# A tile scheduler that models the port between VectorE and GpSimd, small products for two columns, an early table load, and four wide stages

## Chip, core and metric

The kernel runs on one core of a Trainium2 chip. The time is the device time of one execution in microseconds (us), the median over several executions. Lower is better.

## What is computed

An RWKV-style attention feeds a two-layer block with a leaky ReLU. Shapes: 4 batches, 8 heads, 768 steps, head width 48; 3072 tokens of width 384; hidden width 2048.

```python
# attention, for each step t, state starts at zero
cur   = einsum('bhd,bhe->bhde', u[None] * k_t, v_t)
y_t   = einsum('bhd,bhde->bhe', r_t, state + cur)
state = w[None, :, :, None] * state + einsum('bhd,bhe->bhde', k_t, v_t)
# x is y with the heads side by side: [3072, 384]
h = x @ w_in                    # 384 -> 2048
out = maximum(0.01 * h, h) @ w_out   # 2048 -> 384
```

## The kernel before

**Tiling.** The 24 stages (4 batches x 6 chunks of 128 steps) are numbered n = 0 to 23. Stage n is one attention chunk and yields 128 tokens. Inside a chunk the recurrence is written with powers of w: r and k are multiplied by tables (`tab`, L786), scores are taken on TensorE (`sc`, L898), masked on VectorE (`at`, L916), multiplied with v and with the carried state (`y`, L928 and L932), the bonus term with u is added (`ys`, L939), and the new state is formed (`kv` L951/L955, `s` L964). The result is turned to have features on partitions (`yt`, L976, evicted by `xt`, L982; from stage 10 on by a transposing DMA, L987).

**Two forms of a stage.** A plain stage loads r, k and v with 192-byte rows (L619), and multiplies 128x768 in one VectorE instruction (`kq`, L786); eight TensorE transposes (`tp`, L832) give `kt`. The first `NWIDE` = 5 stages are "wide": they are loaded in 1536-byte rows (L617), in an order in which eight consecutive steps of one head lie in one partition. Those need other tables (`tabw`, L582 and L586, made from `lnp`, L578, the logarithm of a narrow load of w, L538), a multiplication for r and one for k (`kw`, L743), a turn of r, k and v by 16 small products each (`turn`, L714), and back-transposes `bk` (L767) and `bv` (L807). In wide stages the bonus comes from a product with the columns `uw` (`pq` L857, `pb` L864, `b` L869/L870, `bv` L873), in plain ones from two GpSimd multiplications and a VectorE reduction (`pu` L880, `pr` L882, `b` L884, `bv` L886).

**Columns.** `wcol` and `uw` hold w and u along partitions. Two ScalarE-queue DMAs load w and u into `wu` (L654, L655) and two fp32 transposes turn them (L600, L601). The ScalarE table load (L1151) stands after those DMAs.

**The hidden block.** `moe_g1` (L1015) multiplies `xT` with `w_in` in blocks of one PSUM bank; `ga` (L1029) evicts a block to `gring`; for every 2 or 4 blocks `gs` makes 0.01*h (L1043 on VectorE, L1044 on ScalarE) and `gm` takes the maximum (L1050, VectorE). `moe_g2` (L1077) multiplies with `w_out` in four quarters per stage; `ob` (L1088, L1089) evicts, and a DMA writes the output (L1094). `GROUPS` says how many stages share one `g1`: single stages 0 to 3, then pairs, and single stages 22 and 23. The last stage's `g2` is cut in 3 column parts.

**What sets the order.** Nothing is written out by hand: `Plan.schedule` (L136) places all operations. Each has an engine or several to choose from (`alt`), a planned duration, dependencies, buffers, and a priority made of its due time and an offset by kind (`POFF`). At each step an engine takes the candidate that can begin first, ties by priority. The engines then run their lists in order, each waiting on semaphores (`sync`, L380). TensorE lists are filled with products of zeros (L1114) where the planner expects idle time before `WARM_UNTIL` = 20 us. `Plan.execute` (L260) replays the lists with a model of the DMA queues for the planned landing times. `DMA_SEQ` writes the order of the first loads: `st2@r0` issues the loads of stage 2 once r of stage 0 has landed; `wi0`, `wi1` are the two halves of w_in and `wo0` to `wo2` the parts of w_out, on GpSimd's queue.

Of the kernel before, what the change touches and what calls it, by code (L numbers as in the profile page):

```python
# [6 lines left out]
ALU = mybir.AluOpType  # L7
AF = mybir.ActivationFunctionType
AX = mybir.AxisListType
BF16 = mybir.dt.bfloat16  # L10
# [14 lines left out]
GROUPS = [1, 1, 1, 1, 2, 2, 2, 2, 2, 2, 2, 2, 2, 1, 1]  # L25
# [11 lines left out]
HEAD_SLACK = 0.1  # L37
HEAD = 14.0
POFF = {'pb': -6, 'tab': -6, 'b': 6, 'xt': -12, 'g1': 12, 'bv': 12, 'vw': -1.5, 'vb': -6, 's': -6, 'bdw': 6, 'kv': -12, 'vt': -1.5, 'sc': 1.5, 'af': -12, 'kt': -3, 'kq': 1.5, 'pu': -6, 'tp': -1.5, 'g2': -6, 'ys': -6, 'od': 12, 'at': 1.5, 'tv': 6, 'gs': 3, 'uw': -3, 'bk': 3, 'pr': -6, 'wc': 3, 'ln': -12, 'yt': -6, 'pq': -1.5, 'ob': -1.5}
# [6 lines left out]
WI = [8, 8]  # L46
WO = [4, 4, 8]
DMA_SEQ = 'st0 st1 st2@r0 u@k0 w@r0 st3@k0 wi0@v2 wi1@v3 wo0@u st4@v0 wo1@v0 wo2@r1'
WP_ON = "SP"
NWIDE = 5  # L50
V_WIDE = 5
BONUS_PE = 5
MASK_SPLIT = 0
KT_SPLIT = 2
KQ_SPLIT = 1
GS_POOL = 0
LAST_SPLIT = 3
GA_ALT = 8
# [4 lines left out]
class Op:  # L63

    def __init__(self, eng, took, fn, name, prio):
        self.alts = [(eng, took, fn)]
        self.eng, self.fn, self.name, self.prio = eng, fn, name, prio
        self.deps, self.behind, self.vals, self.new, self.users = set(), set(), [], [], []
        self.pk, self.sem, self.ndma = None, None, 1
        self.start = self.end = self.done = self.pos = self.semval = None  # L70
        self.left = 0
        self.mark = False
        self.snap, self.waits = {}, []
        self.count = 1
# [27 lines left out]
class Plan:  # L102
# [5 lines left out]
    def op(self, eng, took, fn, name, prio, reads=(), writes=(), after=(), pk=None, sem=None, ndma=1,  # L108
           behind=(), joins=(), alt=None):
# [4 lines left out]
        o.pk, o.sem, o.ndma = pk, sem, ndma  # L114
# [21 lines left out]
    def schedule(self, filler, filler_dep, filler_until):  # L136
# [40 lines left out]

        left = len(self.ops)
        while left:
            pick = None  # L180
            for e in ENGS:
                best = None
                for o, al in cand[e]:
# [14 lines left out]
                    if sl is None:  # L198
                        continue
                    key = (max(st, free[e] + (HEAD_SLACK if free[e] < HEAD else SLACK)), o.prio)  # L200
# [34 lines left out]
            free[e] = o.end  # L235
            if o.pk is not None:
                if o.name in self.landing:
                    o.done = o.end + self.landing[o.name] + (MARGIN if o.name[:2] in ("ld", "wi", "wo") else 0.0)
                else:
                    dma_free[0] = max(o.end + 1.0, dma_free[0]) + o.pk[0] * o.pk[1] / 16000.0  # L240
                    o.done = dma_free[0] + LAND
# [18 lines left out]
    def execute(self, order, case=(1.6, 1.0, 1.1, 2.4, 0.7, 1.0)):  # L260
# [7 lines left out]
        hold = {}  # L268
        now = 0.0
# [14 lines left out]
        def advance():  # L284
            moved = True
            while moved:
                moved = False
                for e, lst in order.items():
                    while nxt_i[e] < len(lst) and e not in hold:
# [23 lines left out]
                        else:  # L313
                            end[o] = st + took - min(HIDE[e], took / 2)
# [5 lines left out]
        def issue(o, e, fin):  # L320
# [3 lines left out]
            begin[o] = fin + (gap_w if e == "POOL" else gap_h if heavy else gap_l + (0.0 if any(x in end for x in dmaq[e][:1] if x is not o) else 0.5))  # L324
# [96 lines left out]
def bass_rwkv5_eagle__then__act_leaky_relu_kernel(  # L421
# [13 lines left out]
    def SB(name, shape, dt=BF16):  # L435
        return ctx.enter_context(nc.sbuf_tensor(name, shape, dt))
# [12 lines left out]
    lnw = SB("lnw", [128, H, D], FP32)  # L449
    lnp = SB("lnp", [128, D], FP32)  # L450
# [5 lines left out]
    wu = SB("wu", [HP, 2, 2, 64], FP32)  # L456
    id4 = SB("id4", [HP, HP], FP32)
# [47 lines left out]
    def build(landing):  # L505
# [17 lines left out]
        def pr_a(n, x=0.0):  # L523
            return (n - LEAD) * PERIOD + x

        f_ones, f_tri, f_idn, f_bd, f_zer, f_uw, f_bdw, f_wc, f_wc2, f_lnw, f_lnw2, f_u, f_wu, f_id4 = [
            fixed(x) for x in ("ones", "tri", "idn", "bd", "zer", "uw", "bdw", "wc", "wc2", "lnw", "lnw2", "u", "wu", "id4")]
# [6 lines left out]
        f_lnp, f_lnp2, f_row, f_rowf = [fixed(x) for x in ("lnp", "lnp2", "row", "rowf")]  # L534
        f_cj = [fixed(f"cj{x}") for x in range(2)]
        f_tabw = [[fixed(f"tabw{i}{x}") for x in range(2)] for i in range(2)]
        if NWIDE:
            o_wp = op(WP_ON, 0.7, lambda: [ENG[WP_ON].dma_start(lnp[:, :], dram(w, 0, [[0, 16], [D, H], [1, D]]))],  # L538
                      "wp", -201, writes=[f_lnp], pk=(128, 16.3), sem="wp")
        o_zer = op("DVE", 0.2, lambda: V.memset(zer[:, :], 0.0), "zer", -200, writes=[f_zer])  # L540
        op("DVE", 0.17, lambda: V.memset(ones[:, :], 1.0), "ones", -199, writes=[f_ones])
        op("DVE", 0.17, lambda: V.memset(wu[:, 0, :, :], 1.0), "wu0", -198, writes=[f_wu])
        op("DVE", 0.17, lambda: V.memset(wu[:, 1, :, :], 0.0), "wu1", -197, joins=[f_wu])
        op("DVE", 0.07, lambda: V.memset(id4[:, :], 1.0), "id40", -196, writes=[f_id4])
        for i, (base, mul) in enumerate([(-L, 1), (L - 1, -1), (0, 1), (-1, -1)]):
# [9 lines left out]
        op("POOL", 0.15, lambda: G.affine_select(id4[:, :], id4[:, :], pattern=[[1, HP]], compare_op=ALU.is_equal,  # L555
                                                 fill=0.0, base=0, channel_multiplier=-1),
           "id4", -193, writes=[f_id4])
# [6 lines left out]
        if NWIDE:  # L564
# [13 lines left out]
            op("ACT", 0.2, lambda: A.activation(lnp[:, :], lnp[:, :], AF.Ln), "lnp", -196, reads=[f_lnp], writes=[f_lnp2])  # L578
            for i in range(min(2, NWIDE)):
                for x in range(2):  # L580
                    def mtw(eng, i=i, x=x):
# [3 lines left out]
                       reads=[f_lnp2, f_cj[x]], writes=[f_tabw[i][x]], alt=("POOL", 1.1, (lambda mtw=mtw: mtw(G))) if i else None)  # L585
# [13 lines left out]
        def go_tuw():  # L599
            PE.transpose(puw.t[:, 0:HP], wu[:, 0, :, :].rearrange("p a d -> p (a d)"), id4[:, :])  # L600
            return PE.transpose(puw.t[:, HP:2 * HP], wu[:, 1, :, :].rearrange("p a d -> p (a d)"), id4[:, :])  # L601
# [3 lines left out]
        def load(n, prio, after=()):  # L605
# [3 lines left out]
            for xi, (nm, src) in enumerate((("r", r), ("k", k), ("v", v))):  # L609
                fv = fixed(f"{nm}{n}")  # L610

                wide = n < NWIDE and (xi < 2 or n < V_WIDE)
# [40 lines left out]
        def go_wu():  # L653
            return [A.dma_start(wu[:, 0, :, 0:D], dram(w, 0, [[2 * D, HP], [D, 2], [1, D]])),  # L654
                    A.dma_start(wu[:, 1, :, 0:D], dram(u, 0, [[2 * D, HP], [D, 2], [1, D]]))]  # L655
        op("ACT", 1.4, go_wu, "wu", -400, writes=[f_wu], pk=(60, 30), ndma=2, sem="wu")
# [39 lines left out]
        op("PE", 0.1, go_tuw, "tuw", -150, reads=[f_wu, f_id4], writes=[puw]).count = 2  # L696
# [11 lines left out]
        op("DVE", 0.56, lambda: mbdw(V), "bdw", -18, reads=[f_bd, f_wc2], writes=[f_bdw], alt=("POOL", 1.1, lambda: mbdw(G)))  # L708
# [16 lines left out]
        def attention(n):  # L725
# [11 lines left out]
            if n < NWIDE:  # L737
                kw_ = new("kw", n)
                for x in range(2):
                    kws = {"writes": [kw_]} if x == 0 else {"joins": [kw_]}  # L740

                    def mw(eng, x=x):
# [4 lines left out]
                            reads=[(f_r, f_k)[x], f_tabw[l][x]], alt=("POOL", 1.15, (lambda mw=mw: mw(G))) if n else None, **kws)  # L747
# [13 lines left out]
                bk = bank(f"a_bk{n}")  # L761

                def go_bk():
                    o = None
                    tv = bk.t[:, :].bitcast(BF16)
                    for i in range(HP):
                        o = PE.transpose(tv[:, 128 * i:128 * i + 128], kt.t[:, HP + i, :], idn[:, :])  # L767
                    return o
                q = op("PE", 0.22, go_bk, f"bk{n}", pr_a(n, 0.47), reads=[f_idn], writes=[bk], after=[ev])
                q.count = HP  # L770
                kt.readers.append(q)

                def cpb(e):
                    o_ap = kq.t[:, H:2 * H, :].rearrange("p h e -> p (h e)")
                    i_ap = bk.t[:, :].bitcast(BF16)[:, 0:512]
                    return V.tensor_copy(o_ap, i_ap) if e == "DVE" else A.activation(o_ap, i_ap, AF.Copy)
                op("DVE", 0.42, lambda: cpb("DVE"), f"kq{n}", pr_a(n, 0.48), reads=[bk] + f_pad, writes=[kq],
                   alt=("ACT", 0.6, lambda: cpb("ACT")))
            elif n < KQ_SPLIT:
                for x in range(2):  # L780
# [3 lines left out]
                           f"kq{n}_{x}", pr_a(n, 0.0), reads=[(f_r, f_k)[x], f_tab[l][x]] + f_pad, **kw))  # L784
            else:
                use(op("DVE", 1.2, lambda: V.tensor_tensor(kq.t[:, :, 0:D], vr.t[:, 0:2, :, :].rearrange("p a h d -> p (a h) d"),  # L786
                                                           tab[l][:, :, :, :].rearrange("p a h d -> p (a h) d"), ALU.mult),
                       f"kq{n}", pr_a(n, 0.0), reads=[f_r, f_k] + f_tab[l] + f_pad, writes=[kq]))
            vb = new("vb", n)
            if n < NWIDE and n < V_WIDE:  # L790
                vw, vt, tv_, bv_ = new("vw", n), new("vt", n), bank(f"a_tv{n}"), bank(f"a_bv{n}")
                def cw(e):
# [4 lines left out]
                       alt=[("DVE", 0.35, lambda: cw(V)), ("POOL", 0.7, lambda: cw(G))]))  # L797
# [56 lines left out]
            if n < max(BONUS_PE, NWIDE):  # L854
                pq, pb = new("pq", n), bank(f"a_pb{n}")
                def mpq(eng):
                    return eng.tensor_tensor(pq.t[:, :, :], kt.t[:, 0:HP, :], kt.t[:, HP:2 * HP, :], ALU.mult)  # L857
                op("DVE", 0.48, lambda: mpq(V), f"pq{n}", pr_a(n, 0.38), reads=[kt], writes=[pq],
                   alt=("POOL", 1.4, lambda: mpq(G)))
# [12 lines left out]
                def mbv(eng):  # L872
# [4 lines left out]
                   alt=("POOL", 1.1, lambda: mbv(G)))  # L877
            else:
                pu, pr, bb = new("pu", n), new("pr", n), new("b", n)
                use(op("POOL", 1.15, lambda: G.tensor_tensor(pu.t[:, :, :], vr.t[:, 1, :, :], ubc[:, :, :], ALU.mult),  # L880
                       f"pu{n}", pr_a(n, 0.2), reads=[f_k, f_u], writes=[pu]))
                use(op("POOL", 1.15, lambda: G.tensor_tensor(pr.t[:, :, :], pu.t[:, :, :], vr.t[:, 0, :, :], ALU.mult),  # L882
                       f"pr{n}", pr_a(n, 0.3), reads=[f_r, pu], writes=[pr]))
                op("DVE", 0.54, lambda: V.tensor_reduce(bb.t[:, :], pr.t[:, :, :], AX.X, ALU.add),  # L884
                   f"b{n}", pr_a(n, 0.8), reads=[pr], writes=[bb])
                op("POOL", 1.1, lambda: G.tensor_tensor(bv.t[:, :].rearrange("p (h d) -> p h d", d=D),  # L886
                                                        vb.t[:, :].rearrange("p (h d) -> p h d", d=D),
                                                        bb.t[:, :].unsqueeze(2).to_broadcast([128, H, D]), ALU.mult),
                   f"bv{n}", pr_a(n, 0.4), reads=[vb, bb], writes=[bv])
# [100 lines left out]
        def moe_g1(n0, T):  # L990
# [16 lines left out]
            for j in range(NFB // per):  # L1007
# [25 lines left out]
                if j % nu == nu - 1:  # L1033
# [12 lines left out]
                    def mx(j0=j0, j=j, hv=hv):  # L1046
# [4 lines left out]
                    op("DVE", 0.79 if nu == 4 else 0.46, (lambda sc=sc: sc("DVE")), f"gs_{n0}_{j}", pr + 0.07,  # L1051
                       after=parts[-nu:], writes=[hv],
                       alt=[("ACT", 1.92 if nu == 4 else 1.06, (lambda sc=sc: sc("ACT")))]
                       + ([("POOL", 2.6 if nu == 4 else 1.4, (lambda sc=sc: sc("POOL")))] if n0 < GS_POOL else []))
                    m = op("DVE", 1.38 if nu == 4 else 0.76, mx, f"gm_{n0}_{j}", pr + 0.08, reads=[hv], after=parts[-nu:])
# [163 lines left out]
```

## Time and profile before

| | |
|---|---|
| median of 5 runs | 182.13 us (181.94 to 182.59) |
| the profiled execution's own time | 182.85 us |
| span of that execution, first to last instruction | 181.1 us |
| mean granted TensorE clock | 0.981 |
| busy: TensorE, VectorE, ScalarE, GpSimd | 171.2, 154.7, 114.9, 82.5 us |
| first `g1` product (L1015) begins | 27.52 us |
| last TensorE product ends | 178.7 us |
| DMA moved | 28.07 MB, mean 155 GB/s |

The profile is of one execution. A line of the groups gives source line, engine, operation, output and input tiles, count, busy time and mean time of one. The timeline lists instructions by start and length; consecutive ones can overlap by their fill and drain, so distances between starts are what one costs its engine. "Idle before" names what ended a wait. Products of zeros count as TensorE busy time.

### The profile page before, as it was taken

How to read it: one execution, taken by the hardware profiler on the slowest of the kernel's cores; microseconds unless marked ns; L12 is line 12 of the kernel's file. 1: busy time of each engine (PE TensorE's matmuls, PEld its weight loads, DVE VectorE, ACT ScalarE, POOL GpSimd, SP SyncE). 2: the span in 40 equal slices, each digit the busy share in tenths (PEclk: the TensorE clock that was granted, in tenths of full speed). 3: DMA queues.
4: the chain of work that ended last, by engine and by line, in shares of the span. 5: the costliest groups of instructions: out<-in, count | busy, mean ns of one | idle time of the engine just before them, and what ended most of it. 6: DMA issues, size and time to landing. Idle time of an engine off the chain costs nothing.

```text
span 181.1 us, 4983 instructions
## 1 busy us (share of the span) xinstructions
PE 171.2 (95%) x2084; PEld 134.3 (74%) x2084; DVE 154.7 (85%) x225; ACT 114.9 (63%) x175; POOL 82.5 (46%) x88
## 2 busy tenths in 40 slices
PE   7388998999999999999999999999999999999994
PEld 3266677976796957877887797778777779686974
DVE  4898896798899999799989879899999969577892
ACT  1648868854599874987856967586637628900350
POOL 3696731043759868568446454552760710000000
PEclk9859999999999999999999999999999999999999
DMA  3869999789981479979979888969978461120202
GB/s 96 275 184 268 209 206 212 151 161 190 265 184 22 91 167 197 209 149 149 254 148 158 216 159 203 203 130 250 191 164 182 88 161 22 25 87 0 91 0 87
DMA packets 88686, 28.07 MB, mean 155 GB/s; under 512 B 81880, under 2 KB 87384, under 8 KB 88664
## 3 DMA queue, kind: packets, MB, share of 16 engines
q1 hardware_dynamic: 83536, 19.89, 53.7%
q0 software_dynamic: 1360, 3.15, 9.1%
q10 hardware_dynamic: 3768, 4.72, 7.6%
q8 instruction: 16, 0.26, 0.6%
q14 instruction: 6, 0.05, 0.1%
HBM read 20.87 MB, written 4.72 MB: 141 GB/s over the span
## 4 chain that ended last, share of the span: by engine, by line
PE 77%; DVE 16%; issue 4%; ACT 1%; ACTq 0%; DVEq 0%
PE ps_g L1077 32%; PE ps_g L1015 30%; DVE at L916 4%; PE ps_xy L898 4%; PE ps_g L932 2%; DVE gring L1050 2%; PE ps_g L714 2%; PE ps_st L955 2%; DVE kq L786 2%; PE ps_g L928 2%; DVE s L964 1%; DVE tabw L582 1%; DVE y L939 1%; DVE kw L743 1%; DVE h L1043 1%
## 5 line engine op out<-in xcount | busy, mean ns | idle before, releaser
L1015 PE MATMUL ps_g<-xT,win 128*128 128x256 bf16 (+1 forms) x720 | 70.8, 251 | 0.8 <-issue 0.8
L1077 PE MATMUL ps_g<-wout,gring 128*128 128x384 bf16 (+1 forms) x416 | 69.3, 314 | 0.1
L1015 PEld LDWEIGHTS ps_g<-xT,win 128*128 128x128 bf16 x720 | 62.7, 114 | 3.0 <-issue 1.0
L1029 ACT ACTIVATE gring<-ps_g 128x512 bf16<-128x512 f32 x72 | 40.8, 597 | 20.6 <-PE ps_g L1015 19.7
L1077 PEld LDWEIGHTS ps_g<-wout,gring 128*128 128x128 bf16 x416 | 36.7, 98 | 20.4 <-DVE gring L1050 0.3
L1044 ACT ACTIVATE h<-gring 128x2048 bf16<-128x2048 bf16 (+1 forms) x25 | 40.1, 1607 | 14.5 <-DVE gring L1029 14.0
L1050 DVE TENSOR_TENSOR gring<-gring,h 128x2048 bf16<-128x2048 bf16 (+1 forms) x30 | 35.5, 1188 | 2.8 <-ACT h L1044 2.5
L886 POOL TENSOR_TENSOR bv<-vb,b 128x384 bf16<-128x384 bf16 x19 | 18.4, 966 | 42.0 <-DVE b L884 33.8
L916 DVE TENSOR_TENSOR at<-ps_xy,tri 128x1024 bf16<-128x1024 f32 x24 | 29.2, 1217 | 4.9 <-PE ps_xy L898 4.9
L882 POOL TENSOR_TENSOR pr<-pu,raw 128x384 f32<-128x384 f32 x19 | 26.8, 1410 | 1.3
L880 POOL TENSOR_TENSOR pu<-raw,ubc 128x384 f32<-128x384 f32 x19 | 20.4, 1076 | 10.3 <-DMA raw<-in_k_dram 10.3
L786 DVE TENSOR_TENSOR kq<-raw,tab 128x768 bf16<-128x768 f32 x19 | 21.0, 1105 | 0.0
L1029 DVE CAST gring<-ps_g 128x512 bf16<-128x512 f32 x24 | 16.3, 690 | 3.1 <-PE ps_g L1015 2.6
L1088 ACT ACTIVATE o<-ps_g 128x384 f32<-128x384 f32 x15 | 7.3, 489 | 14.8 <-PE ps_g L1077 14.8
L939 DVE TENSOR_TENSOR y<-ps_g,bv 128x384 bf16<-128x384 f32 x24 | 13.1, 548 | 0.4 <-PE ps_g L932 0.3
L884 DVE TENSOR_REDUCE b<-pr 128x8 f32<-128x384 f32 x19 | 10.3, 542 | 0.1
L818 ACT ACTIVATE vb<-raw 128x384 bf16<-128x384 f32 x19 | 9.9, 522 | 0.0
L898 PE MATMUL ps_xy<-kt 48*128 48x128 bf16 x192 | 9.7, 222 | 0.0
L1089 DVE COPY o<-ps_g 128x384 f32<-128x384 f32 (+1 forms) x11 | 5.3, 485 | 5.0 <-PE ps_g L1077 4.9
L898 PEld LDWEIGHTS ps_xy<-kt 48*128 48x128 bf16 x192 | 5.5, 95 | 5.1 <-issue 2.4
L932 PE MATMUL ps_g<-vb,at 128*128 128x48 bf16 x192 | 8.8, 183 | 0.0
L743 POOL TENSOR_TENSOR kw<-raw,tabw 128x384 bf16<-128x384 f32 x7 | 7.7, 1124 | 0.8 <-ACT tabw L586 0.8
(88 smaller groups left out, 146.7 us busy)
## 6 DMA issues: line engine op xcount, KB each, us to landing
raw<-in_r_dram SPq DMA_DIRECT2D x24, 192.0 KB, 3.6
raw<-in_k_dram SPq DMA_DIRECT2D x24, 192.0 KB, 3.7
raw<-in_v_dram SPq DMA_DIRECT2D x24, 192.0 KB, 3.8
out_dram<-o ACTq DMA_DIRECT2D x23, 192.0 KB, 2.7
win<-in_moe_w_in_dram POOLq DMA_DIRECT2D x2, 768.0 KB, 9.9
wout<-in_moe_w_out_dram POOLq DMA_DIRECT2D x2, 384.0 KB, 11.8
wout<-in_moe_w_out_dram POOLq DMA_DIRECT2D x1, 768.0 KB, 16.0
kt<-kq SPq DMA_TRANSPOSE x15, 3.5
```

Of the source, the lines that this page charges most:

```text
L786: use(op("DVE", 1.2, lambda: V.tensor_tensor(kq.t[:, :, 0:D], vr.t[:, 0:2, :, :].rearrange("p a h d -> p (a h) d"), tab[l][:, :, :, :].rea ...
L880: use(op("POOL", 1.15, lambda: G.tensor_tensor(pu.t[:, :, :], vr.t[:, 1, :, :], ubc[:, :, :], ALU.mult), f"pu{n}", pr_a(n, 0.2), reads=[f_ ...
L882: use(op("POOL", 1.15, lambda: G.tensor_tensor(pr.t[:, :, :], pu.t[:, :, :], vr.t[:, 0, :, :], ALU.mult), f"pr{n}", pr_a(n, 0.3), reads=[f ...
L886: op("POOL", 1.1, lambda: G.tensor_tensor(bv.t[:, :].rearrange("p (h d) -> p h d", d=D), vb.t[:, :].rearrange("p (h d) -> p h d", d=D), bb ...
L898: o = PE.matmul(xy.t[:, 512 * s + 128 * i:512 * s + 128 * i + 128], kt.t[rows, HP + i, :], kt.t[rows, i, :], start=(i == 0), stop=True, sk ...
L916: op("DVE", 1.22, lambda: V.tensor_tensor(at.t[:, :, :], xy.t[:, :].rearrange("p (h t) -> p h t", t=128), tri_b.to_broadcast([128, H, 128] ...
L939: op("DVE", 0.55, lambda: V.tensor_tensor(ys.t[:, :], y.t[:, 0:DM], bv.t[:, :], ALU.add), f"ys{n}", pr_a(n, 0.5), reads=[y, bv], writes=[ys])
L1015: o = PE.matmul(bk.t[:, 128 * T * f:128 * T * (f + 1)], w_in_block(s, j * per + f), xT[:, s, L * n0:L * n0 + L * T], start=(s == 0), stop= ...
L1029: return A.activation(o_ap, i_ap, AF.Copy) if e == "ACT" else V.tensor_copy(o_ap, i_ap)
L1044: return A.activation(o_ap, i_ap, AF.Copy, scale=LRELU_SLOPE)
L1050: return V.tensor_tensor(flat(dst(j0, j + 1)), flat(dst(j0, j + 1)), h_ap, ALU.max)
L1077: o = PE.matmul(bk.t[:, 0:cw], gring[:, n % NG, fb, :], wout[:, fb, cs], start=(fb == 0), stop=(fb == NFB - 1))
```

## The change

Parameters, with those that decide something here:

```diff
-GROUPS = [1, 1, 1, 1, 2, 2, 2, 2, 2, 2, 2, 2, 2, 1, 1]
+GROUPS = [1, 1, 1, 1, 2, 2, 2, 2, 2, 2, 2, 2, 2, 2]
-HEAD_SLACK = 0.1
-HEAD = 14.0
+HEAD_SLACK = 0.3
+HEAD = 20.0
-WI = [8, 8]
+WI = [4, 4, 8]
-DMA_SEQ = 'st0 st1 st2@r0 u@k0 w@r0 st3@k0 wi0@v2 wi1@v3 wo0@u st4@v0 wo1@v0 wo2@r1'
+DMA_SEQ = 'st0 u st1 wi0@r1 st2@v0 wi1@k2 st3@v0 w@r3 st4@r0 wo0@k1 wi2@v2 wo1 wo2@k4 st5@r4'
-NWIDE = 5
-V_WIDE = 5
-BONUS_PE = 5
-MASK_SPLIT = 0
-KT_SPLIT = 2
+K_WIDE = 5
+NWIDE = 4
+V_WIDE = 6
+BONUS_PE = 4
+MASK_SPLIT = 1
+KT_SPLIT = 5
-GS_POOL = 0
+GS_POOL = 24
-GA_ALT = 8
+GA_ALT = 16
```

`POFF` gets other offsets. With `NWIDE` = 4, `K_WIDE` and `V_WIDE` above it select nothing: all of r, k and v of stages 0 to 3 are wide, stage 4 is plain.

The planner gets a lock. Operations of VectorE and GpSimd that read SBUF with two inputs, and some copies, carry `lock=True`; one begins, in the plan, only after the last one placed on the other engine has ended. Planned durations of many of them are shorter than before.

```diff
+        port = [0.0]
...
+                    if o.lock and e in ("DVE", "POOL"):
+                        st = max(st, port[0])
...
+            if o.lock and e in ("DVE", "POOL"):
+                port[0] = max(port[0], o.end)
```

`execute` gets the same lock, with gaps between earlier uses that a later one may take. No instruction is added on the chip for it; only the lists change.

The columns: w is taken from the narrow load (`lnr`, now 64 columns wide, the last 16 set to 1), u from one DMA of 8 rows, and four fp32 products with an 8x8 identity replace the two transposes. The logarithm now goes from `lnr` to `lnp`.

```diff
-            PE.transpose(puw.t[:, 0:HP], wu[:, 0, :, :].rearrange("p a d -> p (a d)"), id4[:, :])
-            return PE.transpose(puw.t[:, HP:2 * HP], wu[:, 1, :, :].rearrange("p a d -> p (a d)"), id4[:, :])
+            o = None
+            for x, src in enumerate((lnr[0:H, :], up[:, :])):
+                for s in range(2):
+                    o = PE.matmul(puw.t[64 * s:64 * s + 64, HP * x:HP * x + HP], src, id8[:, s:H:2],
+                                  start=(x == 0), stop=True, skip_group_check=True)
+            return o
...
-        op("ACT", 1.4, go_wu, "wu", -400, writes=[f_wu], pk=(60, 30), ndma=2, sem="wu")
+        op("ACT", 0.65, lambda: [A.dma_start(up[:, 0:D], dram(u, 0, [[D, H], [1, D]]))], "up", -400, writes=[f_up],
+           pk=(8, 30), sem="up")
```

The u DMA writes columns that no memset touches, so it waits for none; the two of before waited for the memsets of `wu` (L542, L543). The table load follows it on ScalarE.

How the lists move, by counting the instructions that both kernels issue: the first `g1` product stands on TensorE after `y` of stage 2 (before: after `y` of stage 3). All four `tabw` multiplications are on VectorE (before: three, and one on GpSimd). GpSimd gets 3 `kw` (before 7), 2 `pq` (1), 2 of the 0.01*h (0) and the lower half of stage 0's mask. The logarithm of the wide w load and the four `tab` (L689, L692) stand on ScalarE behind the first `ga`. The first `g2` product stands 8 blocks of `g1` after the first `g1`; the first that needs `wo2` stands 16 blocks after it. The number of products of zeros goes from 32 to 40, small products of `turn` from 240 to 192, `bk` and `bv` transposes from 40 to 32, `tp` transposes from 32 to 40.

## The prediction

> **What bounds the kernel now.** I read the page first, then the chain of waits, then the timelines of VectorE and ScalarE up to 30 us, the busy time by stretches, and the DMA issues.
>
> ```profile
> span 181.1 us, 4983 instructions
> PE 171.2 (95%) x2084; PEld 134.3 (74%) x2084; DVE 154.7 (85%) x225; ACT 114.9 (63%) x175; POOL 82.5 (46%) x88
> PE   7388998999999999999999999999999999999994
> DVE  4898896798899999799989879899999969577892
> PEclk9859999999999999999999999999999999999999
> ```
>
> TensorE is the bound from the eighth slice on; before it stand products of zeros, waits and, in the third slice, half clock. So the time is TensorE's work plus what it loses, and the loss lies mostly in the first 30 us. VectorE comes next, and is full in the middle:
>
> ```profile
> 50.00:60.00 10.00, 9.78 (x130) 8.11 (x128) 10.00 (x13) 10.00 (x15) 7.21 (x7) 1.00 0.40 86
> 60.00:80.00 20.00, 19.84 (x215) 15.41 (x213) 18.68 (x25) 15.43 (x24) 14.01 (x13) 1.00 0.82 168
> ```
>
> (Columns: stretch, length, busy TensorE, weight loads, VectorE, ScalarE, GpSimd, clock, DMA share, GB/s.) VectorE has 10.00 of 10 us there while TensorE waits 0.2: the two are in balance at 50 to 65 us.
>
> From the chain of waits I take what TensorE's work costs:
>
> ```profile
> 26.50 0.36 PE ps_g L714 x16
> 26.86 0.33 PE ps_xy L898 x8
> 155.04 5.20 PE ps_g L1077 x32
> 160.24 2.62 PE ps_g L1015 x24
> 168.73 4.02 PE ps_g L1015 x72
> ```
>
> So 16 small turns cost 0.36, a quarter of `g2` 5.20/8 = 0.65, a 256-wide `g1` product 0.109, a 128-wide one 0.0558. Distances in TensorE's timeline give 0.23 for four back-transposes, 0.10 for the bonus products, 0.45 for eight `tp`, 0.37 for `y`, 0.17 for `kv`. Counting each list without its zeros: 158.5 us of work, 12.5 of them ahead of the first `g1` at 27.52. So 15.0 us are lost by then, 5 more up to the last product at 178.7, and 2.4 follow (eviction, output DMA): 158.5 + 15.0 + 5.2 + 2.4 = 181.1.
>
> **Part 1: TensorE's work.** A wide stage costs 3 x 0.36 + 2 x 0.23 + 0.10 = 1.64, a plain one 0.45: one wide stage less saves 1.2. Stages 22 and 23 as a pair: 48 x 0.109 = 5.24 for 96 x 0.0558 = 5.36, saves 0.1. Two more fp32 products of the columns (rows of 0.20 to 0.22) cost 0.1 to 0.4, in the head where TensorE waits. Sum -1.2: 157.3. This is certain as far as TensorE stays the bound.
>
> **Part 2: the start.** VectorE's first real work waits for ScalarE's logarithm:
>
> ```profile
> 2.98 0.65 ACTq L655 DMA_DIRECT2D wu<-in_u_dram  x1
> 3.65 1.28 ACT L1151 ACT_TABLE_LOAD   x1 [3.65 <-DVE bd L561]
> 4.95 0.24 ACT L578 ACTIVATE lnp<-lnp 128x48 f32<-128x48 f32 x1
> ```
>
> The table load stands behind two DMA issues (the first at 1.71, after the memsets of `wu`), not behind the load of w. With one issue that waits for no memset (from about 0.8, as SP's first does) the table is in by about 2.8. Then w decides: issued from 0.80 to 1.48, 2.2 to landing, so 3.0 to 3.7. I take 3.7: the logarithm comes 1.25 earlier, and can't come over 1.9 earlier. The Trainium skill speaks against this gain: "ScalarE: Activation LUTs", section What ACT_TABLE_LOAD costs, counts a drain of about 1.38 us after the 1.28 us load; by it the table would be in at about 4.2 and the gain 0.7. The row shows the logarithm 0.02 us after the load's end, so here I go by the row.
>
> Then VectorE runs into GpSimd:
>
> ```profile
> 5.22 2.43 DVE L582 TENSOR_TENSOR tabw<-cj,lnp 128x384 f32<-128x384 f32 x3 [2.23 <-ACT lnp L578]
> 7.65 0.54 DVE L743 TENSOR_TENSOR kw<-raw,tabw 128x384 bf16<-128x384 f32 x1
> 8.38 1.09 DVE L743 TENSOR_TENSOR kw<-raw,tabw 128x384 bf16<-128x384 f32 x1
> 9.39 1.35 DVE L706 TENSOR_TENSOR bdw<-bd,wcol 128x384 f32<-128x384 f32 x1
> ```
>
> The same `kw` takes 0.54 alone and 1.09 while GpSimd multiplies (its four `kw` fill 8.00 to 12.74). An undisturbed one costs 0.47 from start to start. In the list of after GpSimd has nothing to multiply until k of stage 1 lands, so VectorE's 4 `tabw` (1.9), small ones (0.45), 2 `kw` (0.95), `bdw` (0.5) take 3.75 for 5.45: the first copy of `kt` stands at about 8.0 for 10.67, 2.7 earlier (1.25 and 1.5). TensorE must be there: its first turns follow the `kw` at 6.9 and 7.4, before at 8.25 and 9.52.
>
> **Part 3: one stage less before the first g1.** Masks of stages 0 to 4 begin at 12.54, 16.26, 19.80, 23.73, 27.64: 3.8 a stage, with VectorE 83 to 100% busy. The first `g1` now needs `y` of stage 2, not 3: -3.8. First `g1` at 27.52 - 2.7 - 3.8 = 21.0, with 9.4 of work done: 11.6 lost for 15.0. If all of it is kept: 3.4 + 1.2 = 4.6.
>
> What else moves in the head: the load of u goes ahead of stage 1 (one issue, 0.6 us; r of stage 1 lands near 8.4, VectorE wants it at 8.5). GpSimd issues five weight DMAs (0.6 to 0.95 each) among three `kw` and the small ops, its `kw` of stage 3 come after four of them, some 5 us before TensorE turns them. The logarithm and four `tab` (5 starts of about 0.5, 2.7) come after the first `g1` eviction on ScalarE; behind them are seven evictions, and TensorE has four blocks' banks and about 1.9 us of attention to cover that. The split mask of stage 0 takes 0.55 off VectorE and adds a 0.5 copy to ScalarE and a select to GpSimd. These I cost at nothing; uncovered, each is 0.5 to 1.
>
> **Part 4: what VectorE gives back.** I add VectorE's list by start distances (`kq` 1.0, mask 1.13, `s`, `y`, `bv`, `kw` 0.47, evictions 0.61, maximum 0.8 or 1.32). Up to the mask of stage 7 it is 41.9 before and 44.4 after: five `kq` for four, four more `kt` and `vt` evictions net of the plain ones, three more `xT` copies, less five `vb`. TensorE's work up to `y` of stage 7 is 42.3 and 42.9. Before, that mask ended at 58.8: start 5.2, work 41.9, 11.7 lost to waits and collisions. After: start 4.0, work 44.4, 11.7 less the head's 1.85 = 9.9: 58.3. Then TensorE reaches `y` 7 having lost 15.7 for 17.1, a gain of 1.4 + 1.2 = 2.6. That is the lower end; the upper is 4.6, when the waits in VectorE's 11.7 (5.8 idle in rows, mostly for TensorE and loads) shrink with TensorE's lead. I take 3.3, nearer to the lower because VectorE's rows are full in 50 to 60. After stage 12 the list leaves TensorE the bound again in both.
>
> **Part 5: the end.** The last pair evicts and scales four blocks at once: 0.61 + 1.1 + 1.38 after the last product, for 0.69 + 0.43 + 0.69 before; TensorE has 2.6 us of other `g2` to lay beside 3.2. Cost 0.4, between 0 and 1.5.
>
> Sum: -3.3 + 0.4 = -2.9. Span 178.2, own time 179.95 from 182.85 (1.75 lie around the span). The median shown is 0.72 below that execution, so 182.13 - 2.9 = 179.2.
>
> **Rivals.**
> - *VectorE doesn't bind; the whole lead is kept.* For it: the head's collisions are gone and 5.8 of VectorE's loss were waits. Against: 10.00 of 10. -4.6 + 0.4, and a warm clock in the third slice could give 1 more: 177 to 178. Chance 0.25.
> - *The lead is lost in the middle.* The lock is in the plan only; GpSimd has one `pu` and `pr` pair more and two scalings, so collisions (1.75 for a `kq` of 0.94 at 44.84) may be as many elsewhere. Only the 1.2 of work is left: 180.5 to 181.5. Chance 0.17.
> - *Slower: the narrow load of stage 4 starves, and with it `wo2`.* That part of w_out (768 KB) is now issued when k of stage 4 has landed, and GpSimd's queue waits there.
>
> ```profile
> wout<-in_moe_w_out_dram POOLq DMA_DIRECT2D x1, 768.0 KB, 16.0
> raw<-in_r_dram SPq DMA_DIRECT2D x1, 192.0 KB, 17.1
> raw<-in_k_dram SPq DMA_DIRECT2D x1, 192.0 KB, 18.5
> ```
>
> Before, the first plain load took 17 to 18.5 beside the weights. After, it is issued at about 14; 18.5 later is 32.7, and `wo2` 10 (the row of w_in) to 16 later, at 43 to 49. TensorE wants it after 18.3 of work from the first `g1`, at about 40. Slower from a k that lands after about 33: 182 to 187. Against: only 1.9 MB of weights are ahead of it for 3.1, begun 4 us earlier; at the 0.17 MB/us of before they are through by 26. Chance 0.08.
> - The forecast: 178.5 to 180.3, chance 0.5.
>
> **Numbers.** About 0.2% (0.36 us) is what a measurement can tell from no change. Slower by more: 0.07, mostly the load; within: 0.05; faster: 0.88. The range leaves out some 0.07 at each end: 177.0 to 181.6.
>
> **What would show it.** The logarithm at 3.7; first `kt` copy near 8; first `g1` near 21; `wo2` landed before 40; TensorE's waits at 45 to 65 for masks or `xT`; VectorE nearly full there. Wrong if the first `g1` stands after 23, if `bv` or `kw` on GpSimd collide as before, or if TensorE waits on a weight load.

## The result, and the profile after

| | before | after |
|---|---|---|
| median of all executions | 182.54 us (71) | 183.21 us (36) |
| lowest and highest | 181.58, 184.82 | 181.31, 186.94 |
| the profiled execution's own time, its span | 182.85, 181.1 | 182.78, 181.0 |

The ratio after to before is 0.9997, 95% interval 0.9978 to 1.0016: no difference that can be measured. (Executions over 1.5% above the fastest of their kernel are left out of every ratio here, 11 of the changed kernel's 36 and up to 4 of 6 in the experiments, so the tables below give the median of all executions beside the ratio.) By the medians of all, the changed kernel is 0.7 us slower. The forecast of 179.2 us and its range, 177.0 to 181.6, miss it.

The page of the changed kernel, the lines that answer to the first fence of before:

```profile
span 181.0 us, 4806 instructions
PE 170.9 (94%) x1998; PEld 132.0 (73%) x1998; DVE 153.7 (85%) x223; ACT 114.1 (63%) x171; POOL 95.8 (53%) x90
PE   7996999999999999999898897999899999999994
DVE  6989988798899989978786676999999989599682
PEclk9999999999999999999999999999999999999999
```

The third slice's half clock is gone and TensorE is full from the fifth slice on; but slices 20, 22, 23, 25 and 29 now have gaps (8 or 7), where the kernel before was full. GpSimd has 13 us more to do.

The start of the changed kernel in ScalarE's timeline, then VectorE's:

```profile
0.78 0.58 ACTq L677 DMA_DIRECT2D up<-in_u_dram  x1
1.40 1.28 ACT L1196 ACT_TABLE_LOAD   x1 [1.40 <-PEq L1249]
2.99 0.24 ACT L598 ACTIVATE lnp<-lnr 128x48 f32<-128x48 f32 x1 [0.31 <-DMA lnr<-in_w_dram]
```

```profile
3.27 1.97 DVE L602 TENSOR_TENSOR tabw<-cj,lnp 128x384 f32<-128x384 f32 x4 [0.27 <-ACT lnp L598]
5.61 1.02 DVE L765 TENSOR_TENSOR kw<-raw,tabw 128x384 bf16<-128x384 f32 x2
6.54 0.55 DVE L728 TENSOR_TENSOR bdw<-bd,wcol 128x384 f32<-128x384 f32 x1
7.27 0.69 DVE L743 CAST kt<-ps_g 128x512 bf16<-128x512 f32 x1 [0.18 <-PE ps_g L736]
```

The logarithm now waits for w only, no multiplication collides, and the first `kt` copy stands 3.4 us earlier than before (10.67). The first `g1` product begins at 21.15 (27.52 before). The `y` of stage 7 stands at 55.78 (59.06). The `kt` copy and the `y` before, and the first `g1` and the `y` after:

```profile
10.67 0.68 DVE L721 CAST kt<-ps_g 128x512 bf16<-128x512 f32 x1
59.06 0.36 PE L932 MATMUL ps_g<-vb,at 128*128 128x48 bf16 x8
```

```profile
21.15 0.86 PE L1060 MATMUL ps_g<-xT,win 128*128 128x128 bf16 x12
55.78 0.36 PE L977 MATMUL ps_g<-vb,at 128*128 128x48 bf16 x8
```

So the lead is made. It can be read as the busy time that TensorE still has ahead of it: 137.9 us before and 134.3 after from 40 us on, 98.3 and 94.5 from 80 on, 38.7 and 38.4 from 140 on. The lead is 3.7 us at 40, 3.8 at 80 and 0.3 at 140. The busy time by stretches (columns as in the prediction: length, busy TensorE, weight loads, VectorE, ScalarE, GpSimd, clock, DMA share, GB/s) shows where it goes. The kernel before:

```profile
80.00:100.00 20.00, 20.00 (x203) 15.89 (x200) 18.67 (x23) 13.85 (x19) 12.41 (x11) 1.00 0.99 183
100.00:120.00 20.00, 20.00 (x206) 16.11 (x205) 17.36 (x23) 14.30 (x22) 9.69 (x9) 1.00 0.86 189
120.00:140.00 20.00, 19.61 (x196) 14.89 (x192) 19.15 (x24) 12.98 (x20) 9.29 (x9) 1.00 0.84 188
```

The changed kernel:

```profile
60.00:80.00 20.00, 20.00 (x214) 15.40 (x213) 18.75 (x24) 14.37 (x23) 17.38 (x12) 1.00 0.81 176
80.00:100.00 20.00, 18.52 (x194) 14.84 (x191) 14.69 (x20) 14.11 (x21) 10.39 (x9) 1.00 1.01 159
100.00:120.00 20.00, 18.63 (x187) 13.85 (x189) 15.60 (x17) 14.72 (x23) 15.65 (x11) 1.00 1.00 184
120.00:140.00 20.00, 18.94 (x185) 13.58 (x181) 19.89 (x23) 11.76 (x18) 10.83 (x10) 1.00 0.86 183
```

From 80 to 140 us TensorE works 59.6 of 60 us before and 56.1 after: 3.5 us, nearly the whole lead, lost far behind the place where the prediction looked. VectorE does not fill this stretch at first (14.69 and 15.60 of 20); only at 120 to 140 is it full. The chain of waits of the changed kernel (start, length, what) names three holders:

```profile
81.17 5.63 DMA kt<-kq
...
92.78 6.68 DMA raw<-in_v_dram
...
108.20 5.37 POOL h L1088
113.60 2.02 DVE gring L1095
115.62 1.13 DVE at L961
```

Two are transfers (the DMA share is 1.0 there); the third is one of the two scalings of h that `GS_POOL` gives to GpSimd.

### The profile page after: what moved, and what is told of

It is laid out like the page before. It is cut to its first block, busy times and chain, and to the rows that moved or that the text cites. A ratio compares the mean times of both kernels' runs of the same rounds, so it can differ in the third digit from the quotient of the medians.

```text
span 181.0 us, 4806 instructions
## 1 busy us (share of the span) xinstructions
PE 170.9 (94%) x1998; PEld 132.0 (73%) x1998; DVE 153.7 (85%) x223; ACT 114.1 (63%) x171; POOL 95.8 (53%) x90
## 4 chain that ended last, share of the span: by engine, by line
PE 54%; DVE 22%; DMA 7%; issue 6%; ACT 5%; POOL 5%; SPq 1%; POOLq 0%
PE ps_g L1122 23%; PE ps_g L1060 18%; DVE gring L1095 6%; DVE kq L831 4%; DMA raw<-in_v_dram 4%; DVE at L961 3%; DMA kt<-kq 3%; POOL h L1088 3%; PE ps_xy L943 3%; PE ps_g L977 2%; DVE gring L1074 2%; ACT h L1089 2%; DVE s L1009 1%; PE ps_g L877 1%; DVE kw L765 1%
## 5 line engine op out<-in xcount | busy, mean ns | idle before, releaser
L1074 ACT ACTIVATE gring<-ps_g 128x512 bf16<-128x512 f32 x76 | 42.4, 595 | 18.3 <-PE ps_g L1060 15.3
L1089 ACT ACTIVATE h<-gring 128x2048 bf16<-128x2048 bf16 (+1 forms) x22 | 38.6, 1754 | 7.4 <-DVE gring L1074 7.0
L1095 DVE TENSOR_TENSOR gring<-gring,h 128x2048 bf16<-128x2048 bf16 (+1 forms) x28 | 34.7, 1239 | 3.3 <-ACT h L1089 2.2
L931 POOL TENSOR_TENSOR bv<-vb,b 128x384 bf16<-128x384 bf16 x20 | 21.4, 1071 | 22.9 <-DVE b L929 22.9
L961 DVE TENSOR_TENSOR at<-ps_xy,tri 128x1024 bf16<-128x1024 f32 x23 | 28.0, 1218 | 4.7 <-PE ps_xy L943 4.7
L925 POOL TENSOR_TENSOR pu<-raw,ubc 128x384 f32<-128x384 f32 x20 | 26.3, 1317 | 10.2 <-DMA raw<-in_k_dram 10.1
L831 DVE TENSOR_TENSOR kq<-raw,tab 128x768 bf16<-128x768 f32 x20 | 24.6, 1231 | 1.9 <-DMA raw<-in_k_dram 1.9
L1133 ACT ACTIVATE o<-ps_g 128x384 f32<-128x384 f32 (+1 forms) x14 | 6.7, 475 | 25.8 <-PE ps_g L1122 25.8
L1074 DVE CAST gring<-ps_g 128x512 bf16<-128x512 f32 x20 | 13.2, 688 | 0.5 <-PE ps_g L1060 0.2
L1134 DVE COPY o<-ps_g 128x384 f32<-128x384 f32 (+1 forms) x12 | 6.2, 513 | 6.4 <-PE ps_g L1122 6.3
L1088 POOL TENSOR_SCALAR h<-gring 128x1024 bf16<-128x1024 bf16 (+1 forms) x2 | 8.1, 4070 | 0.9 <-ACT gring L1074 0.9
```

The costliest lines, as they stand in the source:

```text
L831: use(op("DVE", 0.95, lambda: V.tensor_tensor(kq.t[:, :, 0:D], vr.t[:, 0:2, :, :].rearrange("p a h d -> p (a h) d"), tab[l][:, :, :, :].re ...
L925: use(op("POOL", 1.0, lambda: G.tensor_tensor(pu.t[:, :, :], vr.t[:, 1, :, :], ubc[:, :, :], ALU.mult), f"pu{n}", pr_a(n, 0.2), reads=[f_k ...
L931: op("POOL", 0.83, lambda: G.tensor_tensor(bv.t[:, :].rearrange("p (h d) -> p h d", d=D), vb.t[:, :].rearrange("p (h d) -> p h d", d=D), b ...
L961: op("DVE", 1.22, lambda: V.tensor_tensor(at.t[:, :, :], xy.t[:, :].rearrange("p (h t) -> p h t", t=128), tri_b.to_broadcast([128, H, 128] ...
L1074: return A.activation(o_ap, i_ap, AF.Copy) if e == "ACT" else V.tensor_copy(o_ap, i_ap)
L1088: return ENG[e].tensor_scalar(o_ap, i_ap, LRELU_SLOPE, None, ALU.mult)
```

## The experiments

Theory 1: the loads and transposes, on DMA engines now full from 80 to 120 us, hold TensorE. Theory 2: the GpSimd scaling does, by its late result or by the time that GpSimd is occupied. Theory 3, the prediction's rival: VectorE and GpSimd collide as often as before, only elsewhere. Below, a us figure is the ratio less one, times 182.5. "Lists kept" means that the edit is made after planning, so that every engine's order stays but for the edited instructions.

**Scalings to ScalarE, fewer packets, both, and the control.** e1 and e4, ahead of `P.sync(order)`:

```diff
+    for o in [x for x in order["POOL"] if x.name.startswith("gs_")]:
+        order["POOL"].remove(o)
+        o.eng, o.fn = "ACT", o.alts[1][2]
+        at = sum(x.start <= o.start for x in order["ACT"])
+        order["ACT"].insert(at, o)
```

e2, e3 and e4, in the loads (planned packets unchanged):

```diff
-                    if wide:
+                    if wide or n >= 8:
```

> The changed kernel with its two GpSimd scalings of h (one of 1024, one of 2048 columns) handed to ScalarE at the same planned moments; all other lists stay as they are. Theory 1 (loads: from 80 to 120 us TensorE waits for what the 16 DMA engines, then full, bring late; 2.5 of its 3.9 us of waits there): the scalings are not the cause, time within 0.5 us of the changed kernel, about equal to before. Theory 2 (the scaling of 5.36 us on GpSimd at 108 us delays a maximum and pushes multiplications into collisions; VectorE is full from 113 to 140 us behind it): 1.0 to 2.0 us faster than before. Theory 3 (collisions of VectorE and GpSimd in general, as many as before): under 0.7 us faster.

> The changed kernel with the loads of stages 8 to 23 in 1536-byte rows: the same bytes in an eighth of the packets, all lists and plans unchanged. The values arrive in another order, so from stage 8 on it computes something else with the same instructions. Theory 1: the waits for the transposed kt (0.5 us at 87), for v (1.0 at 100) and for xT (1.0 at 112) go, 2 to 3 us faster than before. Theory 2: no gain over 0.7 us, since GpSimd's scaling still takes over 5 us. Theory 3: no gain over 0.7 us.

> The kernel before with the same loads in 1536-byte rows from stage 8 on (it too then computes something else). TensorE waits for no DMA there from 60 us on (one wait of 0.4 for a mask), so every theory expects within 0.4 us of the kernel before; more would mean that full DMA engines cost time in some other way (slower evictions or matmuls).

> The edits of both together: scalings on ScalarE and loads from stage 8 on in 1536-byte rows (computes something else from stage 8 on). Theory 1: as with the loads alone, 2 to 3 us faster than before. If theories 1 and 2 each hold a part: 3 to 4 us faster, the lead of 4 to 5 us that stood at 78 us, less the tail. Theory 3: under 1 us faster, VectorE full and TensorE waiting for masks from 80 to 140 us.

| kernel | ratio to before | 95% interval | median of all (before 182.52) |
|---|---|---|---|
| e1 scalings on ScalarE | 0.9885 (-2.1 us) | 0.9848 to 0.9923 | 182.02 |
| e2 few packets, after | 0.9964 (-0.7) | 0.9933 to 0.9996 | 182.27 |
| e3 few packets, before | 0.9996 | 0.9957 to 1.0036 | 182.94 |
| e4 both edits | 0.9860 (-2.6) | 0.9801 to 0.9919 | 180.82 |

By its ratio Theory 2 is right in its size; by the medians of all, e1 is 0.5 us faster than before and 1.2 faster than the changed kernel, since six of its twelve executions took 182.5 us or more. One of these is the profiled one (183.08): TensorE worked 56.3 of the 60 us from 80 to 140 there, no more than with the scalings on GpSimd, and waited for a transposed `xT`:

```profile
PE ps_g L1060 <- DMA xT<-y: 2.1, 2, 1.5
```

So the lead can be lost without the scalings too. Theory 1 expected 2 to 3 us of the loads and got 0.7: the waits for DMA in that profile are gone, but TensorE then meets the next limit (it waits 1.8 us for the maximum, L1095, in e2's profile). The loads cost nothing that can be measured before (e3), where TensorE was not ahead of them. Whether they cost anything beside e1 isn't shown: the intervals of e1 and e4 overlap.

**The larger scaling alone; GpSimd occupied without a result to wait for; two new plans.** e5 limits e1's loop to the 2048-column scaling. e6 adds to e1, in the freed places of GpSimd's list:

```diff
+        d = Op("POOL", 2.6, (lambda cols=cols: G.tensor_scalar(idle[:, 0:cols], win[:, 0, 0:cols], LRELU_SLOPE, None, ALU.mult)),
+               "idle", o.prio)
```

e7 and e8 plan anew, e8 without the lock:

```diff
-GS_POOL = 24
+GS_POOL = 0
...
-        o.pk, o.sem, o.ndma, o.lock = pk, sem, ndma, lock
+        o.pk, o.sem, o.ndma, o.lock = pk, sem, ndma, False
```

> The changed kernel with only the larger of GpSimd's two scalings (2048 columns, 5.36 us at 108 us) handed to ScalarE, the smaller one (1024 columns, 2.78 us at 41 us) left on GpSimd, all other lists kept. If the price found with both (about 2 us) is that of the larger, whose result a maximum on VectorE waits 0.95 us for: 1.5 to 2.2 us faster than before. If the smaller one in the full middle costs as much (GpSimd is busy 17 of 20 us at 40 to 60): about 1 us faster. If it all comes from the smaller one: within 0.4 us of before.

> Both scalings on ScalarE as in the first experiment, and in their old places on GpSimd two scalings of the same sizes that read w_in and write a tile that nobody reads (work added, result unchanged). If the price is the wait for the late result (a maximum and the g2 products behind it): 1.5 us faster than before or more, as in the first experiment. If it is GpSimd's time and the collisions during it (its multiplications and bv come 2.8 and 5.4 us later, VectorE's slow down): within 0.5 us of before.

> The changed kernel with GS_POOL = 0, planned anew: GpSimd gets no scaling, and the lists of the middle come out otherwise. Theory 2: 1 to 2.5 us faster than before, 180 to 181.5 us. Theory 3 (collisions as many as before whatever the scalings): under 0.7 us faster. A new plan can move the time by some 0.5 us either way by itself.

> As the run before, with the lock of VectorE and GpSimd taken out of planner and replay, planned anew. If the lock keeps collisions out of the lists: more collisions on VectorE and GpSimd (kq, pu, pr above 1.2, 1.3, 1.35 us in the mean), 0.5 to 2 us slower than the run before. If the lock exists only in the plan (theory 3): within 0.5 us of it, with equal means.

| kernel | ratio to before | 95% interval | median of all (before 182.73) |
|---|---|---|---|
| e5 larger scaling to ScalarE | 0.9925 (-1.4 us) | 0.9896 to 0.9955 | 181.56 |
| e6 idle scalings | 0.9944 (-1.0) | 0.9913 to 0.9975 | 181.37 |
| e7 no scaling, new plan | 1.0057 (+1.0) | 1.0023 to 1.0090 | 184.45 |
| e8 no scaling, no lock, new plan | 1.0025 (+0.5) | 0.9993 to 1.0057 | 182.84 |

The larger scaling is most of it; the smaller one's share isn't told apart from none (e1 and e5 overlap). By the ratio e6 stands between: part is the late result, part perhaps the occupied time. By the medians of all, e6 is 1.4 us faster than before and so ahead of e1. e7 missed: without scalings, but in another order, the lead is lost again. In e7's profile (182.01 us, its fastest execution) TensorE waits 1.1 us for a `vb` and 0.9 for a transposed `kt`. The lock thins out collisions of `kq` (1135 ns in the mean in e7, 1332 in e8), but not those of the maximum (1233 and 1160) or of GpSimd's `pr` (1478 and 1390), and the time is no better for it.

**The new plan with fewer packets; the two ends of the head; e1 again.** e9 is e7 with e2's edit. e10 changes one line of the kernel before, e11 adds to e1 three copies ahead of the logarithm:

```diff
-            if not loaded and o.pk is None:
+            if not loaded:
```

```diff
+    first = next(o for o in order["ACT"] if o.name == "lnp")
+    at = order["ACT"].index(first)
+    for i in range(3):
+        d = Op("ACT", 0.5, lambda i=i: A.activation(idle[:, 512 * i:512 * i + 512], zer[:, :], AF.Copy), "idle", 0)
+        ...
+        order["ACT"].insert(at + i, d)
```

> The re-planned kernel without GpSimd's scalings (GS_POOL = 0), its lists kept, with the loads of stages 8 to 23 in 1536-byte rows (values in another order, so it computes something else from stage 8 on). In that plan TensorE lost 2.2 us at 100 to 120 us, where it waited 1.1 us for a vb and 0.9 us for a transposed kt. If the loads and transposes beside one another cost that plan its gain: 1.5 to 2.5 us faster than the re-planned kernel, so 0.5 to 1.5 us faster than before. If it is its order on VectorE: within 0.5 us of the re-planned kernel, 1 us slower than before.

> The kernel before with one thing of the change: ScalarE's table load stands ahead of its two narrow DMA issues instead of behind them; all lists are otherwise those of before. The logarithm should begin when w lands, near 3.7 or sooner, for 4.95 us; the columns' DMAs come 1.3 us later. If an earlier start of VectorE's head is worth its time at the end: 0.4 to 1.2 us faster than before. If the columns' delay takes it back, or the middle does: within 0.4 us.

> The changed kernel with both scalings on ScalarE, as in the first experiment, and three copies of 512 columns to a tile that nobody reads put ahead of the logarithm on ScalarE: the logarithm comes about 1.4 us later, near where it was before (work added, result unchanged). If the head's lead is carried to the end once the scalings are off GpSimd: 1.0 to 1.5 us slower than the first experiment, 0.6 to 1.1 us faster than before. If the middle sets the time and swallows it: within 0.5 us of the first experiment.

> The kernel of the first experiment once more (both scalings on ScalarE), beside the others of this call. Expected as measured: 1.4 to 2.8 us faster than before, TensorE waiting under 2.5 us in all from 60 to 160 us. If the first result was chance: within 0.5 us of before.

| kernel | ratio to before | 95% interval | median of all (before 182.80) |
|---|---|---|---|
| e9 new plan, few packets | 0.9922 (-1.4 us) | 0.9873 to 0.9972 | 182.68 |
| e10 before, table first | 0.9970 (-0.5) | 0.9940 to 1.0001 | 182.31 |
| e11 e1 with a late logarithm | 0.9954 (-0.8) | 0.9923 to 0.9984 | 182.29 |
| e12 e1 again | 0.9833 (-3.0; 2 of 6 executions) | 0.9766 to 0.9900 | 182.28 |

In the new plan it is the loads: 2.4 us between e7 and e9 (1.8 by the medians of all). Whether the head's time is carried to the end isn't shown. e11's logarithm comes 1.29 us later than the changed kernel's. By the ratios the time is then 1.3 us longer than e1's, as if it were carried. By the medians of all, e1, e11 and e12 lie together, each 0.5 below before. ScalarE's timelines of e10 and of e11:

```profile
0.80 1.28 ACT L1151 ACT_TABLE_LOAD   x1 [0.80 <-PEq L1204]
1.72 1.23 ACTq L654 DMA_DIRECT2D wu<-in_w_dram  x1
...
3.66 0.24 ACT L578 ACTIVATE lnp<-lnp 128x48 f32<-128x48 f32 x1 [1.58 <-DMA lnp<-in_w_dram]
```

```profile
1.41 1.28 ACT L1209 ACT_TABLE_LOAD   x1 [1.41 <-PEq L1262]
2.70 1.67 ACT L1182 ACTIVATE idle<-zer 128x512 bf16<-128x512 bf16 x3
4.28 0.23 ACT L599 ACTIVATE lnp<-lnr 128x48 f32<-128x48 f32 x1
```

In e10 the logarithm is 1.29 us earlier (in the profiled execution, one of 592.12 us in which TensorE ran slow throughout), and the gain is 0.5, with an interval from 0 to 1.1: what else held that head, this run doesn't settle.

**Late result or occupied time, with the clock kept up.** In the profile of e12 TensorE was busy 1.15 of the 2 us from 16 on, and its granted clock (third figure from the end) then fell to 0.50 at 20 to 22 us:

```profile
16.00:18.00 2.00, 1.15 (x39) 0.91 (x39) 2.00 (x3) 0.28 (x1) 0.78 (x1) 1.00 1.22 211
20.00:22.00 2.00, 2.00 (x34) 1.42 (x30) 1.19 (x3) 1.13 (x3) 0.00 (x0) 0.50 1.12 207
```

The gap alone does not decide it: in the profiles of the changed kernel and of e1 TensorE was busy 1.16 and 1.06 of the same 2 us, and the clock stayed at 1.00. The last four kernels get eleven products of zeros there: e13 is the changed kernel so, e14 is e1 so, e15 is e6, e16 is e4.

```diff
+    for name, num in (("tw2_0", 4), ("tw2_1", 7)):
+        at = next(i for i, o in enumerate(order["PE"]) if o.name == name)
+        ...
+            order["PE"].insert(at, f)
```

> The changed kernel with eleven more products of zeros on TensorE, four ahead of the first and seven ahead of the second turn of stage 2's kw (near 15.0 and 16.0 us, where TensorE waits 0.55 and 0.84 us for VectorE), all lists kept. If they only fill waits: the same time as the changed kernel's undisturbed executions, within 0.4 us of before; the clock 1.0 all the way, so the spread of the executions gets smaller. If they push the turns back: up to 0.5 us slower than before.

> The same with both scalings on ScalarE. As measured without the zeros: 1.5 to 2.8 us faster than before, 179.7 to 181 us, most executions under 181.5; the fastest correct version so far. If the former gain was a matter of which executions were compared: under 1 us faster.

> The same as the run before, with two idle scalings of the same sizes (they read w_in and write a tile that nobody reads) in the old places on GpSimd. If the late result is the price: within 0.5 us of the run before, 1.5 us or more faster than e13. If GpSimd's occupied time and its collisions are: within 0.5 us of e13. In between, the share of each can be read off.

> As e14, with the loads of stages 8 to 23 in 1536-byte rows (values in another order, so it computes something else from stage 8 on). If loads and transposes beside one another still cost TensorE its lead at 80 to 120 us: 0.7 to 1.5 us faster than e14. If VectorE, full at 120 to 140 us, is what is left: within 0.4 us of e14.

| kernel | ratio to before | 95% interval | median of all (before 182.38) |
|---|---|---|---|
| e13 zeros | 1.0047 (+0.9 us) | 1.0016 to 1.0078 | 183.55 |
| e14 zeros, scalings on ScalarE | 0.9905 (-1.7) | 0.9856 to 0.9953 | 182.05 |
| e15 zeros, idle scalings on GpSimd | 0.9939 (-1.1) | 0.9902 to 0.9975 | 181.56 |
| e16 zeros, scalings on ScalarE, few packets | 0.9941 (-1.1) | 0.9909 to 0.9973 | 181.46 |

The clock stayed at 1.00 in all 12 executions of e13 and in 11 of 12 of each other kernel, and the spread of e13 shrank to 182.69 to 184.12; but the zeros cost 0.9 us by the ratios (0.5 by the medians of all). From e13 to e14 the scalings are worth 2.6 us, and 2.0 of it come back while GpSimd is as occupied as before (e15): **the late result is most of the price**. By the medians of all, e14 is 1.5 us faster than e13 and e15 2.0, and e6 is 2.0 faster than the changed kernel when each is set against before, so this holds by either measure. The occupied time is 0.6 by the ratios of e14 and e15 and 1.1 by those of e1 and e6, but by the medians of all the kernels with the occupied GpSimd are the faster ones, by 0.5 and 0.9: that it costs anything isn't shown. e16 and e14 aren't told apart: by the ratios e16 is 0.6 slower, by the medians 0.6 faster.

How a late result costs more than VectorE's wait for it: GpSimd's scaling and VectorE's timeline, first of the changed kernel, then of e15.

```profile
108.20 5.36 POOL L1088 TENSOR_SCALAR h<-gring 128x2048 bf16<-128x2048 bf16 x1
111.18 1.46 DVE L831 TENSOR_TENSOR kq<-raw,tab 128x768 bf16<-128x768 f32 x1
113.60 2.02 DVE L1095 TENSOR_TENSOR gring<-gring,h 128x2048 bf16<-128x2048 bf16 x1 [0.95 <-POOL h L1088]
115.54 1.21 DVE L961 TENSOR_TENSOR at<-ps_xy,tri 128x1024 bf16<-128x1024 f32 x1
```

```profile
107.65 5.37 POOL L1189 TENSOR_SCALAR idle<-win 128x2048 bf16<-128x2048 bf16 x1
110.92 1.18 DVE L832 TENSOR_TENSOR kq<-raw,tab 128x768 bf16<-128x768 f32 x1
112.02 1.21 DVE L1096 TENSOR_TENSOR gring<-gring,h 128x2048 bf16<-128x2048 bf16 x1
113.16 1.21 DVE L962 TENSOR_TENSOR at<-ps_xy,tri 128x1024 bf16<-128x1024 f32 x1
```

The maximum waits 0.95 us, and then runs beside the GpSimd multiplications that had queued up behind the scaling (2.02 for 1.21). The mask of a stage stands behind it in VectorE's list; from the start of `kq` it comes 4.36 us later for 2.24. From there the changed kernel's VectorE is full to 140 us and can't give it back. e15's GpSimd runs the idle scaling all the while (107.65 to 113.02) and delays no one by much.

The profiled execution of e14, the fastest of its twelve, which took 179.44 us in a span of 177.7:

```profile
80.00:100.00 20.00, 20.00 (x209) 16.37 (x208) 15.41 (x21) 15.79 (x22) 11.39 (x9) 1.00 0.94 182
100.00:120.00 20.00, 19.48 (x203) 14.49 (x201) 15.98 (x20) 15.19 (x23) 11.86 (x11) 1.00 0.97 186
120.00:140.00 20.00, 19.39 (x198) 14.59 (x197) 19.48 (x23) 12.23 (x17) 11.36 (x11) 1.00 0.96 185
```

58.9 of 60 us of work, for 59.6 before: the lead is kept but for 0.7. In e15's profiled execution, 181.15 us and near its median, it is 58.6. The forecast for the changed kernel's span was 178.2; of e14's twelve executions only this one comes to it. The changed kernel with its two scalings on ScalarE (e1) is faster than both by either measure, without the zeros, but by how much depends on the measure: 1.2% against before by the ratio (0.8 to 1.5), 0.3% by the medians of all.

## Why the prediction was wrong

- **Part 1, work.** Not shown by itself; nothing contradicts it.
- **Part 2, the start.** Right, and a little too careful. Logarithm at 2.99 (3.7 forecast), first `kt` copy at 7.27 (8.0; the forecast's own terms add up to 7.7). That w lands at 3.0 here and at 3.66 in e10's profiled execution isn't explained. The Trainium skill's "ScalarE: Activation LUTs", section What ACT_TABLE_LOAD costs, was cited for a drain of about 1.38 us behind the load; no run shows one: e11's first copy begins 0.01 after it.
- **Part 3, the first g1.** 21.15 for 21.0, but by two misses that offset one another, so partly by luck: the start was worth 3.4 us for 2.7, the stage less 3.0 for 3.8.
- **Part 4.** It lets VectorE give back 1.3 of a lead of 4.6 by stage 7, and nothing behind that. Both halves are off. The 3.3 that it keeps is a gain of the whole time; by its own sum it puts `y` of stage 7 about 1.5 us earlier (work 42.9 for 42.3, 2.1 lost less). It was 3.3 earlier, and the lead stayed at 3.7 to 3.8 us from 40 to 80: VectorE took nothing there that can be seen. **The step that failed is its last sentence**, "After stage 12 the list leaves TensorE the bound again in both". TensorE lost 3.5 us at 80 to 140, and the end sum took none of it. What the runs show in its place is the late result of the GpSimd scaling in front of a maximum and a mask: 1.0 to 2.0 us. The trace of before has no such scaling on GpSimd, and I bounded it from no side. The rows for it were there: on GpSimd 384 columns take 0.83 to 1.0 us and 512 took 1.15, so 2048 take 4.4 to 5.3, not the planned 2.6; it measured 5.36. And behind its result stand a maximum and a mask. The rest of the 3.5 is shown only in part.
- **Part 5, the end.** The last product still ends 2.4 us ahead of the span's end; its last 64 products take 5.75 us for 5.3 by the rows (16 x 0.163 + 48 x 0.0558), near the 0.4 forecast; the row of before, 4.14, exceeds the same prices by 0.16 too. Not tried by itself.
- **The rivals.** "VectorE doesn't bind; the whole lead is kept" held up to 80 us. "The lead is lost in the middle" came nearest and named the scalings, but put the loss on collisions and left 1.2 us over; it was the late result (1.0 to 2.0 us in the two pairs), perhaps the occupied time (0 to 1.1) and perhaps 0.7 of loads that TensorE had caught up with. Its condition held, and so did a sign named for being wrong, collisions as many as before: from before to after a `kq` went from 1105 to 1231 ns in the mean, `pu` from 1076 to 1317, GpSimd's `bv` from 966 to 1071. What these cost by themselves no run shows; e15, 2.0 us faster than e13, has a `kq` of 1268. In the plans without scalings the lock was worth nothing (e8 against e7). The starving `wo2` did not happen: the page of the changed kernel has it land in 7.7 us, at about 36.8, 3.6 ahead of its use:

```profile
wout<-in_moe_w_out_dram POOLq DMA_DIRECT2D x1, 768.0 KB, 7.7
```

What stays open: the smaller scaling's share; why the zeros cost time; whether the head's time is carried; why half of e1's executions lose the lead without the scalings, with waits for `xT` in the one profiled; and why two orders of nearly the same instructions, e1's and e7's, differ by 3 us by the ratios (2.2 by the medians of all), of which loads explain 2.4 (1.8).

## What to carry to other kernels

A lead at the front is worth its time only if nothing behind it was sized for the old pace: go through the later stages for what the bound engine will now catch up with, loads first. Where a change hands work to a slower engine, scale its time from that engine's own rows by the number of columns, and look at what stands behind the consumer in the consumer's in-order list; the price is that delay, not the consumer's wait. To separate a late result from an occupied engine, give the result to another engine and leave idle work of the same size in the old place.

## What the hardware showed

- GpSimd's multiplication by a constant took 2.6 to 2.7 ns per column in bf16 in the changed kernel (2.78 us for 1024, 5.36 for 2048; the idle one of 1024 took 3.21 in e15); VectorE's scaling of 2048 columns in the changed kernel's tail took 0.69.
- Beside this one-input scaling a maximum and a mask kept their undisturbed length (1.21 and 1.23 in e15), while a `kq` took 1.18 in e15 and 1.46 in the changed kernel for 0.95 undisturbed (e14). Beside GpSimd's two-input multiplications a maximum took 2.02 and a `kq` up to 1.75.
- In e12 TensorE's clock fell to 0.50 some 2 us after a stretch in which it was busy 1.15 of 2 us, and stayed there for 2 to 3 us; after 1.16 of 2 us in the changed kernel and 1.06 in e1 it stayed at 1.00.
